# One piece or two for a pair's weighted sums, with the order of a whole kernel tuned anew

## The chip, the core and the metric

The kernel runs on one core of one Trainium2 chip. The metric is the device time of one execution in microseconds (us); lower is better. A core has TensorE (PE, matmuls; its weight loads are shown as PEld), VectorE (DVE), ScalarE (ACT), GpSimd (POOL) and SyncE (SP, which issues the DMAs here). TensorE writes its results to PSUM, eight banks of 512 fp32 columns on 128 partitions, from which ACT or DVE copies them out.

## The reference

Attention with a multiplicative decay comes first, over 8 batches and 8 heads, with 576 positions and 64 dimensions a head; then a gated layer over the 512 joined columns. All of it is fp32:

```python
scores = scale * np.matmul(q, k.transpose(0, 1, 3, 2))
decay = cum[:, :, :, None] - cum[:, :, None, :]        # cum: running sum of log f
scores = np.where(causal, -1000000000.0, scores + decay)
scores = scores - np.max(scores, axis=-1, keepdims=True)
attn = np.exp(scores)
attn = attn / (np.sum(attn, axis=-1, keepdims=True) + 1e-09)
x = attn @ v                                           # heads joined: (B, S, 512)
gate_pre = sum(conv_w[k] * x_shifted_by(4 - k) for k in range(5))
out = (1 / (1 + np.exp(-gate_pre)) * (x @ w_val)) @ w_out
```

The step of interest is `attn @ v`, the weighted sums of values.

## The kernel before

The 64 heads are taken as 32 pairs (two heads share the 128 partitions, 64 dimensions each); four pairs make a batch. For pair `i` five planning functions run in turn. `plan_t` transposes q and k on TensorE. `plan_s` multiplies them; for each block of rows VectorE adds the decay and finds the maximum (line 604), ScalarE takes the exponential with its row sum (line 608), and one of POOL, DVE or ACT divides by the sum (lines 380 and 382). Only blocks at or below the diagonal are computed. The first 512 rows go by four blocks of 128; the last 64 rows of both heads form one tile `Pl` of 576 columns, whose scores take two adjacent banks. `plan_pt` transposes the weights (lines 649, 667, 668), and copies them to the tiles `pt`. `plan_pv`, the changed function, multiplies the values `vt` with the transposed weights: head h goes to partitions 64h to 64h + 63, so each matmul uses half of the array's columns (128*64 in the trace). Its result x, 128 partitions by 576 positions, is copied to `x32` (class "X"), split in a rounded part `xh` and a rest `xl`, and used for the gate: for the first four pairs by matmuls with diagonal matrices ("CV"), then by five multiplications on VectorE ("conv", line 747). After four pairs `plan_moe` does the batch's sigmoid, the products with `w_val` (class "Mv", in three parts for precision), the product with the gate ("H", line 792), the products with `w_out` ("Mo") and the output copies and stores.

In `plan_pv` before, x is made in two parts, each with a bank of its own and a copy of its own. The first covers positions 0 to 383: 12 products of 128 columns over block rows 0 to 2. The second covers 384 to 575: eight products of 192 columns and two of 64. The profile counts two TensorE instructions for each of these fp32 products, hence 24 and 20. The first part needs the transposed weights named 1 and 2, the second those named 3, l and l4.

None of this is issued in the order in which it is written. Each piece of work is a node of a list (`Plan.add`) with its class, the engines that can do it and an assumed duration for each, its priority, and what it reads and writes. `Plan.order` (line 189) then plays the whole kernel through: again and again it picks the engine and node that can start first, taking from the nodes ready within a small slack (`SLACK`) the one with the lowest priority. The priority is the pair's number plus small steps (`prio`), plus an offset from the table `OFF` for the class and for one of six phases of the kernel (`phase`, line 92). `PEN` adds a penalty where a node could go to several engines; `STICK` favours TensorE work of the same array shape (`mode` 0 full array, 1 half of the rows, 3 half of the columns), and `SWITCH` is the assumed price of a change of shape. PSUM banks are given out here too: a node that first touches a bank waits in the plan until one is free, or two side by side where it asks for `width` 2 (`seize`, `room`), and a bank comes back 0.15 us after its last use. A node that takes a bank also waits for everything that later users of that bank wait for, unless it is marked loose (line 153). The result is one fixed sequence for each engine, kept on the chip; the actual waits there are those of each single instruction on its data and banks.

Of the kernel before, what the change touches and what calls it, by code (L numbers as in the profile page):

```python
# [15 lines left out]
P = 128  # L16
D = 64
S = 576
PAD = 64
W = PAD + S  # L20
NB = 4
# [16 lines left out]
SAME = {"PE": 0.0, "ACT": 0.06, "DVE": 0.1, "POOL": 0.1, "SP": 0.0, "DQ": 0.0}  # L38
SLACK = {"PE": 0.0, "ACT": 0.0, "DVE": 0.0, "POOL": 0.0, "SP": 0.1, "DQ": 0.2}
SWITCH = 0.105  # L40
STICK = 24.84
PORT = {"norm", "conv", "hh", "hl", "xl", "xh", "sel", "wv", "wo", "cw", "start", "st0", "cut0", "cuth", "cutl"}
TICK, BUSY = 10.24 / 3, 3150.0
OFF = {
# [13 lines left out]
    "norm": (-64.92, -34.44, -50.35, -154.2, -42.93, -56.64), "rec": (-34.14, 96.95, -10.49, -75.27, 12.83, -25.56),  # L58
    "red": (5.64, -89.32, -29.74, -47.57, -60.46, -12.2), "sel": (0.99, -66.53, -101.3, -61.6, -6.31, 30.49),
    "sig": (0.0, 0.0, 119.1, 276.6, 80.13, 83.28), "st0": (-101.2, 0.0, 0.0, 0.0, 0.0, 0.0),  # L60
    "start": (-51.51, 0.0, 0.0, 0.0, 0.0, 0.0), "tabD": (-58.73, 0.0, 0.0, 0.0, 0.0, 0.0),
# [4 lines left out]
}  # L66
PEN = {
# [5 lines left out]
    ("conv", "ACT"): (0.0, 0.0, 2.52, 7.5, 4.7, 2.58), ("conv", "DVE"): (0.0, 0.0, 0.38, 0.0, 0.0, 0.5),  # L73
    ("conv", "POOL"): (0.0, 0.0, 65.48, 22.89, 42.2, 42.68), ("cut0", "DVE"): (12.46, 0.0, 0.0, 0.0, 0.0, 0.0),
    ("diag", "DVE"): (0.33, 1.54, 0.91, 0.0, 0.0, 0.0), ("diag", "POOL"): (11.96, 28.56, 14.33, 0.0, 0.0, 0.0),
    ("hh", "ACT"): (0.0, 0.0, 0.06, 0.0, 0.0, 7.62), ("hh", "DVE"): (0.0, 0.0, 0.22, 12.6, 5.06, 1.54),
    ("hl", "DVE"): (0.0, 0.0, 9.17, 0.64, 3.65, 0.0), ("hl", "POOL"): (0.0, 0.0, 0.51, 0.54, 0.04, 22.01),
    ("load", "ACT"): (7.36, 0.0, 0.0, 0.0, 0.0, 0.0), ("load", "SP"): (0.03, 0.0, 0.0, 0.0, 0.0, 0.0),
    ("norm", "ACT"): (0.0, 0.04, 0.67, 0.05, 0.79, 15.64), ("norm", "DVE"): (0.77, 5.49, 22.53, 0.36, 6.39, 2.21),
    ("norm", "POOL"): (3.05, 17.25, 0.28, 44.42, 0.8, 0.08), ("sel", "DVE"): (29.3, 28.29, 53.65, 8.66, 76.26, 0.31),  # L80
    ("sel", "POOL"): (1.34, 0.0, 0.11, 0.0, 0.0, 9.64), ("start", "ACT"): (5.02, 0.0, 0.0, 0.0, 0.0, 0.0),
    ("start", "DVE"): (5.62, 0.0, 0.0, 0.0, 0.0, 0.0), ("start", "POOL"): (0.21, 0.0, 0.0, 0.0, 0.0, 0.0),
# [5 lines left out]
}  # L88
NONE = (0.0,) * 6

# [189 lines left out]
def tile_decay_attention_gated_mlp(  # L280
# [12 lines left out]
    B, H = q.shape[0], q.shape[1]  # L293
# [5 lines left out]
    T0 = KC - 1  # L299
# [14 lines left out]
    cw = const.tile([P, KC, G], F32, name="cw")  # L314
# [10 lines left out]
    pt = tiles(NH, [P, 1600], F32, "pt")  # L325
    vt = tiles(NQ, [P, NB + 1, 2, D], F32, "vt")
# [4 lines left out]
    xh = tiles(NX, [P, S], F32R, "xh")  # L331
    xl = tiles(NX, [P, S], F32R, "xl")
# [3 lines left out]
    hh = tiles(G, [P, W], F32R, "hh")  # L336
    hl = tiles(G, [P, W], F32R, "hl")
# [15 lines left out]
    new = plan.bank  # L353

    def bank(key):
        home = plan.home[key]
        return banks[:, 512 * home[0]:512 * (home[-1] + 1)]

    def mm(out, lhsT, rhs, start, stop):
        nc.tensor.matmul(out, lhsT=lhsT, rhs=rhs, start=start, stop=stop)  # L360
# [8 lines left out]
    dve, act, pool, pe = (one(e) for e in ("DVE", "ACT", "POOL", "PE"))  # L369

    def any_(cls, durs, prio, fn, reads=(), writes=(), **kw):
        return plan.add(cls, durs, prio, lambda e: fn(engine[e]), reads, writes, **kw)

    def copy(eng, out, in_):
        (eng.copy if eng is nc.scalar else eng.tensor_copy)(out=out, in_=in_)  # L375
# [13 lines left out]
    def ap(n):  # L389

        return {"ACT": n / 1200.0 + 0.05, "DVE": n / 960.0 + 0.075}
# [241 lines left out]
    def at(i, j):  # L633
        return 192 * j if i == 3 else (1152, 1280, 768)[i] + P * j
# [47 lines left out]
    def plan_pv(i):  # L682
        b, g = divmod(i, G)
        r = i % NQ
        ms = [(2 * i + h) % NH for h in range(2)]
        base = float(i) if i else -5.0
        xr = x32[r]
        vk = [("vt0", r), *(("vt", r, n) for n in range(3))]
        for half, (qa, qb) in enumerate(((0, 384), (384, 576))):
            key = new(("PV", i, half))  # L690
            p = base + 0.6 + 0.05 * half

            def go(key=key, half=half):
                t = bank(key)
                if half == 0:
                    for bq in range(3):
                        for j in range(bq + 1):
                            for h in range(2):
                                mm(t[D * h:D * h + D, P * bq:P * bq + P], vt[r][:, j, h], pt[ms[h]][:, at(bq, j):at(bq, j) + P], j == 0, j == bq)
                    return  # L700
                for j in range(NB):
                    for h in range(2):
                        mm(t[D * h:D * h + D, 0:192], vt[r][:, j, h], pt[ms[h]][:, 192 * j:192 * j + 192], j == 0, False)
                for h in range(2):
                    mm(t[D * h:D * h + D, P:192], vt[r][:, NB, h], pt[ms[h]][:, 1536:1600], False, True)
            names = ((1, 2), (3, "l", "l4"))[half]
            pe("PV", (1.36, 1.47)[half], p, go, [*vk, *(("pt", m, n) for m in ms for n in names), *(("pt0", m) for m in ms)], [key],
               cols=(6144, 7168)[half], mode=3)

            def ev(eng, key=key, qa=qa, qb=qb):  # L710
                copy(eng, xr[:, T0 + qa:T0 + qb], bank(key)[:, 0:qb - qa])
            any_("X", ap(qb - qa), p, ev, [key], [("x", r, half)])
        xv = xr[:, T0:]
        s = i % NX
        xk = [("x", r, 0), ("x", r, 1)]
        p = base + 0.8
# [224 lines left out]
```

## Time and profile before

| | us |
|---|---|
| median of three runs | 592.03 (588.51 to 593.89) |
| the profiled execution | 589.74 |
| its span, first to last instruction | 588.0 |
| TensorE busy | 566.3 |
| ScalarE busy | 460.9 |
| VectorE busy | 449.9 |
| GpSimd busy | 251.6 |

The profiled execution's time is 1.7 us more than its span. Busy time is the union of an engine's instructions; matmuls overlap one another, so a busy TensorE is not one at its peak. In a row of groups stand line, engine, operation, output and inputs, shape and count, then busy time, mean length in ns, idle time just before and what ended it. In rows of the timeline the first two numbers are start and length in us, `x44` counts merged instructions, and brackets hold the idle time before and its releaser. The granted clock of TensorE was 0.997 of full speed.

### The profile page before, as it was taken

The numbers are of one execution on the slowest core, as the hardware profiler recorded it, in microseconds if no ns is written. First come the engines' busy times: TensorE is split into PE (matmuls) and PEld (weight loads), VectorE is DVE, ScalarE is ACT, GpSimd is POOL, SyncE is SP. The second block draws the span as 40 slices with busy tenths as digits, with TensorE's granted clock in tenths as the row PEclk, the third lists the DMA queues.
The fourth block names the chain that finished last, engine by engine and source line by source line (L and its number), as shares of the span: only waits on it lengthen the run. The fifth ranks groups of instructions, "written<-read, shape, count | busy, mean of one in ns | idle before, by whom it ended". The sixth has DMA issues, their size and how long they took to land.

```text
span 588.0 us, 14152 instructions
## 1 busy us (share of the span) xinstructions
PE 566.3 (96%) x4773; PEld 493.8 (84%) x4773; DVE 449.9 (77%) x1200; ACT 460.9 (78%) x1252; POOL 251.6 (43%) x397
## 2 busy tenths in 40 slices
PE   6798989999999999999999999999999999999997
PEld 5576768888789988889888998989988998889995
DVE  5668969799987989779778888696767778775550
ACT  4979969999987698779898889987887786984201
POOL 5121257333322654553554654343664666371200
PEclk9999999999999999999999999999999999999999
DMA  5999787575754566385667666564666645210002
GB/s 136 258 223 262 167 232 220 155 180 158 232 134 137 147 186 192 116 236 145 174 160 194 173 178 178 166 179 124 171 200 171 169 131 163 81 47 19 37 37 89
DMA packets 136294, 93.44 MB, mean 159 GB/s; under 512 B 118474, under 2 KB 118494, under 8 KB 136222
## 3 DMA queue, kind: packets, MB, share of 16 engines
q1 hardware_dynamic: 136222, 92.54, 57.2%
q8 instruction: 38, 0.62, 0.5%
q14 instruction: 34, 0.28, 0.2%
HBM read 82.60 MB, written 9.91 MB: 157 GB/s over the span
## 4 chain that ended last, share of the span: by engine, by line
PE 70%; DVE 10%; ACT 7%; DMA 7%; issue 2%; SPq 2%; POOL 1%; DVEq 0%; POOLq 0%; ACTq 0%
PE banks L360 56%; PE banks L649 8%; DVE banks L604 4%; ACT P L608 3%; PE banks L530 3%; SPq L387 2%; DVE gate L747 2%; DMA vt<-in_v_dram 2%; PE banks L667 1%; DMA ot<-in_moe_w_out_dram 1%; ACT pt L375 1%; DMA dm<-decd 1%; DMA ot<-in_moe_w_val_dram 1%; DMA wu<-in_moe_w_val_dram 1%; DVE negm L604 1%
## 5 line engine op out<-in xcount | busy, mean ns | idle before, releaser
L608 ACT ACTIVATE P<-banks,negm 128x128 f32<-128x128 f32 (+3 forms) x256 | 132.9, 536 | 26.6 <-DVE negm L604 26.3
L604 DVE CUSTOM_DVE_ANT_0 banks<-banks,dm 128x128 f32<-128x128 f32 (+3 forms) x256 | 120.6, 515 | 30.3 <-PE banks L360 19.1
L375 ACT COPY pt<-banks 128x256 f32<-128x256 f32 (+2 forms) x320 | 115.9, 437 | 28.7 <-PE banks L649 24.2
L382 POOL TENSOR_SCALAR P<-P,rz 128x384 f32<-128x384 f32 (+3 forms) x134 | 79.7, 611 | 73.3 <-DVE rz L618 36.7
L360 PE MATMUL banks<-xh,wall 128*128 128x288 f32 x512 | 108.7, 299 | 1.5 <-ACT pt L375 1.4
L747 DVE SCALAR_TENSOR_TENSOR gate<-x,cw,gate 128x576 f32<-128x576 f32 x112 | 103.0, 920 | 1.8
L360 PE MATMUL banks<-pt,vt 128*64 128x128 f32 (+2 forms) x1408 | 97.0, 293 | 3.5 <-ACT pt L375 2.9
L360 PEld LDWEIGHTS banks<-pt,vt 128*64 128x64 f32 x1408 | 86.0, 138 | 15.6 <-ACT pt L375 4.3
L434 POOL TENSOR_SCALAR_AFFINE_SELECT dm<-dm 128x256 f32<-128x256 f32 x126 | 55.7, 467 | 96.6 <-DMA dm<-decd 90.2
L360 PE MATMUL banks<-wall,hh 128*128 128x512 f32 x288 | 93.0, 404 | 1.1 <-ACT P L608 0.9
L649 PE MATMUL banks<-ident,P 128*128 128x128 f32 x640 | 89.3, 277 | 4.0 <-ACT P L380 1.4
L360 PEld LDWEIGHTS banks<-xh,wall 128*128 128x128 f32 x512 | 83.5, 188 | 3.6 <-ACT pt L375 1.6
L649 PEld LDWEIGHTS banks<-ident,P 128*128 128x128 f32 x640 | 71.3, 140 | 12.2 <-ACT P L380 3.4
L360 PE MATMUL banks<-xl,wall 128*128 128x288 f32 x256 | 75.4, 295 | 0.0
L718 POOL TENSOR_TENSOR xl<-x,xh 128x576 fp32r<-128x576 f32 x32 | 50.6, 1583 | 48.9 <-ACT xh L375 48.9
L360 PEld LDWEIGHTS banks<-wall,hh 128*128 128x128 f32 x288 | 51.0, 188 | 11.7 <-ACT P L608 2.3
L360 PE MATMUL banks<-Xh 128*128 128x288 f32 (+4 forms) x280 | 58.4, 346 | 0.6 <-ACT P L608 0.5
L380 ACT ACTIVATE P<-P,rz 128x128 f32<-128x128 f32 (+3 forms) x114 | 58.2, 574 | 0.6 <-DVE rz L618 0.3
L360 PE MATMUL banks<-wall,hl 128*128 128x512 f32 x144 | 56.5, 392 | 0.0
L608 ACT ACTIVATION_READ_ACCUMULATOR P<-banks,negm 128x1 f32 x256 | 54.1, 211 | 0.0
L360 PE MATMUL banks<-Xh,Xl 128*128 128x288 f32 (+4 forms) x280 | 52.9, 314 | 0.0
L360 PE MATMUL banks<-Xl,Xh 128*128 128x288 f32 (+4 forms) x280 | 52.9, 313 | 0.0
(108 smaller groups left out, 933.3 us busy)
## 6 DMA issues: line engine op xcount, KB each, us to landing
dm<-decd SPq DMA_DIRECT2D x62, 640.0 KB, 5.9
out_dram<-ot SPq DMA_DIRECT2D x36, 256.0 KB, 2.3
dl<-decd SPq DMA_DIRECT2D x62, 144.0 KB, 3.7
qn<-in_q_dram SPq DMA_DIRECT2D x64, 128.0 KB, 2.8
kn<-in_k_dram SPq DMA_DIRECT2D x64, 128.0 KB, 6.3
vt<-in_v_dram SPq DMA_DIRECT2D x64, 128.0 KB, 3.1
zn<-in_q_dram SPq DMA_DIRECT2D x64, 16.0 KB, 3.1
zn<-in_k_dram SPq DMA_DIRECT2D x32, 32.0 KB, 2.8
```

The costliest lines, as they stand in the source:

```text
L360: nc.tensor.matmul(out, lhsT=lhsT, rhs=rhs, start=start, stop=stop)
L375: (eng.copy if eng is nc.scalar else eng.tensor_copy)(out=out, in_=in_)
L380: eng.activation(out=out, in_=in_, func=AF.Copy, scale=col)
L382: eng.tensor_scalar(out=out, in0=in_, scalar1=col, scalar2=0.0, op0=ALU.mult, op1=ALU.add)
L387: lambda e: (nc.sync if e == "SP" else nc.scalar).dma_start(out=out, in_=in_), reads, writes, **kw)
L434: nc.gpsimd.affine_select(out=t, in_=t, pattern=[[0, 2], [-1, P]], base=0, channel_multiplier=1, compare_op=ALU.is_ge, fill=-BIG)
L530: nc.tensor.transpose(out=bank(key)[:, n * P:(n + 1) * P], in_=src[:, n].rearrange("p h d -> p (h d)"), identity=ident)
L604: nc.vector.tensor_tensor_reduce(out=sl, in0=sl, in1=add[:, o:o + ext], op0=ALU.add, op1=ALU.min, scale=-0.125, scalar=3.0e38, accum_out=n ...
L608: nc.scalar.activation(out=dst[:, o:o + ext], in_=bank(key)[:, c0:c0 + ext], func=AF.Exp, bias=negm[r][:, col], scale=-1.0, accum_out=zs[r ...
L649: nc.tensor.transpose(out=bank(key)[:, c:c + P], in_=Pt[m][:, BOFF[b] + P * j:BOFF[b] + P * j + P], identity=ident)
L718: any_("xl", {"POOL": 1.4, "DVE": 0.67}, p, lambda eng: eng.tensor_tensor(out=xl[s], in0=xv, in1=xh[s][:, :].bitcast(F32), op=ALU.subtract ...
L747: eng.scalar_tensor_tensor(out=gt, in0=src, scalar=wt_, in1=gt, op0=ALU.mult, op1=ALU.add)
```

## The change

`plan_pv` makes one node of the two. It takes two adjacent banks and issues all products of the pair, the first part's and then the second's, to a view that starts at column 128 of the first bank: positions 0 to 383 fill that bank to its end, positions 384 to 575 the first 192 columns of the second. The node needs all transposed weights of the pair. One copy of 576 columns, for ACT or DVE, takes the place of the copies of 384 and 192. The assumed duration is 2.83 us, in place of 1.36 and 1.47. The numbers in `OFF`, `PEN` and `STICK`, which set the order, are replaced; a few rows of each table stand here, and the rest change in like manner. `PEN` gains entries such as ("CE", "ACT") and ("wo", "DVE") and loses ("conv", "DVE") and ("xh", "ACT").

```diff
-STICK = 24.84
+STICK = 23.54
...
-    "PT": (-42.2, 16.09, 19.11, 32.94, 6.68, 4.69), "PV": (-64.38, -24.3, 4.98, -25.87, -4.65, -72.64),
-    "S": (-48.98, -34.14, -48.85, -16.38, -24.39, -84.23), "SD": (146.1, 0.0, 0.0, 0.0, 0.0, 0.0),
-    "SX": (-75.7, -6.93, -12.7, 13.98, -13.66, 16.23), "T": (9.34, 83.08, -47.66, 3.31, -17.01, -77.97),
...
+    "PT": (-32.85, 31.08, 19.24, 34.11, -0.14, -0.33), "PV": (-75.34, -39.69, 2.88, -42.73, -13.14, -71.15),
+    "S": (-46.82, -37.29, -29.72, -8.51, -40.34, -65.96), "SD": (152.9, 0.0, 0.0, 0.0, 0.0, 0.0),
+    "SX": (-65.95, 2.57, 5.45, 27.72, -7.91, 13.86), "T": (-44.11, 47.99, -87.47, -36.81, -52.52, -90.14),
...
-        for half, (qa, qb) in enumerate(((0, 384), (384, 576))):
-            key = new(("PV", i, half))
-            p = base + 0.6 + 0.05 * half
-
-            def go(key=key, half=half):
-                t = bank(key)
-                if half == 0:
-                    for bq in range(3):
-                        for j in range(bq + 1):
-                            for h in range(2):
-                                mm(t[D * h:D * h + D, P * bq:P * bq + P], vt[r][:, j, h], pt[ms[h]][:, at(bq, j):at(bq, j) + P], j == 0, j == bq)
-                    return
-                for j in range(NB):
+        key = new(("PV", i), 2)
+
+        def go(key=key):
+            t = bank(key)[:, P:]
+            for bq in range(3):
+                for j in range(bq + 1):
                     for h in range(2):
-                        mm(t[D * h:D * h + D, 0:192], vt[r][:, j, h], pt[ms[h]][:, 192 * j:192 * j + 192], j == 0, False)
+                        mm(t[D * h:D * h + D, P * bq:P * bq + P], vt[r][:, j, h], pt[ms[h]][:, at(bq, j):at(bq, j) + P], j == 0, j == bq)
+            for j in range(NB):
                 for h in range(2):
-                    mm(t[D * h:D * h + D, P:192], vt[r][:, NB, h], pt[ms[h]][:, 1536:1600], False, True)
-            names = ((1, 2), (3, "l", "l4"))[half]
-            pe("PV", (1.36, 1.47)[half], p, go, [*vk, *(("pt", m, n) for m in ms for n in names), *(("pt0", m) for m in ms)], [key],
-               cols=(6144, 7168)[half], mode=3)
-
-            def ev(eng, key=key, qa=qa, qb=qb):
-                copy(eng, xr[:, T0 + qa:T0 + qb], bank(key)[:, 0:qb - qa])
-            any_("X", ap(qb - qa), p, ev, [key], [("x", r, half)])
+                    mm(t[D * h:D * h + D, 384:576], vt[r][:, j, h], pt[ms[h]][:, 192 * j:192 * j + 192], j == 0, False)
+            for h in range(2):
+                mm(t[D * h:D * h + D, 512:576], vt[r][:, NB, h], pt[ms[h]][:, 1536:1600], False, True)
+        pe("PV", 2.83, base + 0.65, go, [*vk, *(("pt", m, n) for m in ms for n in (1, 2, 3, "l", "l4")), *(("pt0", m) for m in ms)], [key],
+           cols=13312, mode=3)
+        any_("X", ap(S), base + 0.65, lambda eng, key=key: copy(eng, xr[:, T0:], bank(key)[:, P:P + S]), [key], [("x", r, 0), ("x", r, 1)])
```

More of the change, by code (lines that the diff above doesn't have):

```diff
@@ L44 @@
 OFF = {
[13 rows of a table removed]
[L58 to L61, printed above, removed]
[4 rows of a table removed]
[13 rows of a table added]
+    "norm": (-65.73, -57.4, -65.73, -164.1, -38.95, -65.45), "rec": (-58.37, 108.0, 10.25, -97.03, -2.44, -45.11),
@@ L66 @@
+    "red": (0.27, -73.65, -8.48, -64.28, -77.03, -3.12), "sel": (10.54, -34.61, -71.32, -48.15, 32.8, 54.18),
+    "sig": (0.0, 0.0, 98.36, 271.1, 101.0, 78.47), "st0": (-84.38, 0.0, 0.0, 0.0, 0.0, 0.0),
+    "start": (-69.3, 0.0, 0.0, 0.0, 0.0, 0.0), "tabD": (-41.76, 0.0, 0.0, 0.0, 0.0, 0.0),
[4 rows of a table added]
 }
 PEN = {
[5 rows of a table removed]
-    ("conv", "ACT"): (0.0, 0.0, 2.52, 7.5, 4.7, 2.58), ("conv", "DVE"): (0.0, 0.0, 0.38, 0.0, 0.0, 0.5),
-    ("conv", "POOL"): (0.0, 0.0, 65.48, 22.89, 42.2, 42.68), ("cut0", "DVE"): (12.46, 0.0, 0.0, 0.0, 0.0, 0.0),
@@ L75 @@
[L75 to L79, printed above, removed]
@@ L80 @@
-    ("norm", "POOL"): (3.05, 17.25, 0.28, 44.42, 0.8, 0.08), ("sel", "DVE"): (29.3, 28.29, 53.65, 8.66, 76.26, 0.31),
-    ("sel", "POOL"): (1.34, 0.0, 0.11, 0.0, 0.0, 9.64), ("start", "ACT"): (5.02, 0.0, 0.0, 0.0, 0.0, 0.0),
-    ("start", "DVE"): (5.62, 0.0, 0.0, 0.0, 0.0, 0.0), ("start", "POOL"): (0.21, 0.0, 0.0, 0.0, 0.0, 0.0),
[5 rows of a table removed]
[5 rows of a table added]
+    ("X", "DVE"): (2.13, 4.94, 35.86, 32.05, 0.71, 57.96), ("conv", "ACT"): (0.0, 0.0, 9.25, 9.3, 13.41, 4.22),
+    ("conv", "POOL"): (0.0, 0.0, 40.76, 4.31, 25.15, 41.53), ("cut0", "ACT"): (1.28, 0.0, 0.0, 0.0, 0.0, 0.0),
@@ new lines @@
+    ("cut0", "DVE"): (2.31, 0.0, 0.0, 0.0, 0.0, 0.0), ("diag", "DVE"): (0.92, 0.72, 0.04, 0.0, 0.0, 0.0),
+    ("diag", "POOL"): (16.29, 20.59, 11.74, 0.0, 0.0, 0.0), ("hh", "ACT"): (0.0, 0.0, 0.1, 0.14, 0.34, 0.75),
+    ("hh", "DVE"): (0.0, 0.0, 0.24, 8.42, 0.0, 0.0), ("hl", "DVE"): (0.0, 0.0, 8.88, 0.06, 5.67, 0.0),
+    ("hl", "POOL"): (0.0, 0.0, 0.31, 5.35, 0.65, 19.45), ("load", "ACT"): (4.84, 0.0, 0.0, 0.0, 0.0, 0.0),
+    ("norm", "ACT"): (0.0, 0.0, 0.83, 0.34, 1.19, 19.16), ("norm", "DVE"): (0.88, 7.08, 32.18, 0.41, 7.67, 8.27),
@@ L88 @@
+    ("norm", "POOL"): (6.91, 21.31, 0.17, 41.53, 0.77, 0.2), ("sel", "DVE"): (20.36, 31.89, 58.03, 8.15, 74.04, 11.84),
+    ("sel", "POOL"): (0.11, 0.9, 0.0, 0.01, 0.0, 0.0), ("start", "ACT"): (3.27, 0.0, 0.0, 0.0, 0.0, 0.0),
+    ("start", "DVE"): (5.56, 0.0, 0.0, 0.0, 0.0, 0.0), ("start", "POOL"): (1.17, 0.0, 0.0, 0.0, 0.0, 0.0),
[5 rows of a table added]
 }
```

48 rows, old and new, of tables (OFF, PEN) are left out of this document.

## The prediction

> **What bounds the kernel now.** I read the page first (busy shares and the chain), then the busy time by stage, then the groups that the change touches, then TensorE's own timeline around them, and last the waits and the tail.
>
> ```profile
> span 588.0 us, 14152 instructions
> PE 566.3 (96%) x4773; PEld 493.8 (84%) x4773; DVE 449.9 (77%) x1200; ACT 460.9 (78%) x1252; POOL 251.6 (43%) x397
> ...
> PE 70%; DVE 10%; ACT 7%; DMA 7%; issue 2%; SPq 2%; POOL 1%; DVEq 0%; POOLq 0%; ACTq 0%
> ```
>
> TensorE (PE) is the busiest engine and holds 70% of the chain that ended last. An average over stages can deceive, so the stages come next (columns: length, then busy time of each engine with its instruction count, then TensorE's granted clock, the DMA share, GB/s).
>
> ```profile
> 0.00:30.00 30.00, 21.50 (x148) 16.42 (x150) 18.75 (x52) 20.56 (x53) 9.36 (x31) 0.98 0.77 197
> 30.00:116.00 86.00, 80.58 (x624) 63.76 (x621) 68.08 (x206) 74.91 (x207) 34.31 (x59) 0.99 0.79 208
> 116.00:560.00 444.00, 439.95 (x3882) 392.78 (x3881) 355.49 (x923) 361.28 (x987) 207.95 (x307) 1.00 0.55 153
> 560.00:588.00 28.00, 24.27 (x127) 20.82 (x126) 7.59 (x21) 4.11 (x7) 0.00 (x0) 1.00 0.18 66
> ```
>
> There are two regimes. From 116 to 560 us TensorE is busy for 439.95 of 444.00 us at full clock, so 4.05 us of idle time is all that a better order could take from idling; ScalarE (ACT) and VectorE (DVE) are at 81% and 80% there and set nothing by their sums. Before 116 us TensorE idles 8.50 + 5.42 us, and ACT is busy for 74.91 of 86 us between 30 and 116. The last 28 us are matmuls of the output projection and the final copy and store.
>
> **The change part by part.** The work on the pair's weighted sums is in these groups (line 360 is the helper that issues all matmuls, line 375 the helper that copies; the last row is another copy by the same line, for its duration).
>
> ```profile
> L360 PE MATMUL banks<-pt,vt 128*64 128x128 f32 x768 | 49.1, 277 | 3.4 <-ACT pt L375 2.9 <-DVE gate L375 0.5
> L360 PE MATMUL banks<-pt,vt 128*64 128x192 f32 x512 | 48.7, 334 | 0.0
> L360 PE MATMUL banks<-pt,vt 128*64 128x64 f32 x128 | 9.3, 223 | 0.0
> L375 ACT COPY x<-banks 128x384 f32<-128x384 f32 x32 | 15.5, 483 | 7.3 <-PE banks L360 7.1
> L375 ACT COPY x<-banks 128x192 f32<-128x192 f32 x32 | 10.3, 323 | 10.7 <-PE banks L360 10.5
> L375 ACT COPY pt<-banks 128x512 f32<-128x512 f32 x128 | 74.4, 597 | 17.0 <-PE banks L649 16.3
> ```
>
> *Matmuls.* The diff issues the same products with the same operands and sizes: 24 + 20 instructions a pair (768/32, and (512 + 128)/32). The view starts at column 128 of the first bank, so the first 384 columns end exactly at the bank's end and the other 192 begin the second bank. No matmul is added or dropped; the term is 0. What can change is whether the two parts run back to back. TensorE's timeline (start, length, line, group, count) has both forms:
>
> ```profile
> 52.65 1.53 PE L360 MATMUL banks<-pt,vt 128*64 128x128 f32 x24 [0.53 <-DVE gate L375]
> 55.75 1.64 PE L360 MATMUL banks<-pt,vt 128*64 128x192 f32 x20
> ...
> 105.49 1.53 PE L360 MATMUL banks<-pt,vt 128*64 128x128 f32 x24
> 112.99 1.64 PE L360 MATMUL banks<-pt,vt 128*64 128x192 f32 x20
> ...
> 189.69 2.95 PE L360 MATMUL banks<-pt,vt 128*64 128x128 f32 x44
> ...
> 472.37 1.53 PE L360 MATMUL banks<-pt,vt 128*64 128x128 f32 x24
> 480.46 1.64 PE L360 MATMUL banks<-pt,vt 128*64 128x192 f32 x20
> ...
> 527.48 2.94 PE L360 MATMUL banks<-pt,vt 128*64 128x128 f32 x44
> ```
>
> Apart, the parts take 1.53 + 1.64 = 3.17 us, together 2.95: a split costs 0.22 us. But the order before already joins them in 27 of the 32 pairs. Only five are split: four between 52.65 and 112.99 us, and the one at 472.37. So "in one piece" is worth 1 x 0.22 us in the dense stage, and at most 4 x 0.22 = 0.88 us before 116 us.
>
> In those four early pairs the join can also cost. The first part now waits for what the second needs (the transposed weights 3, l and l4), so 1.5 us of work moves later, by up to 7.5 us (105.49 to 112.99), and leaves TensorE without that filler. If nothing else is ready it costs 4 x 1.53 = 6.1 us; if something is, nothing. TensorE idles in this stage anyway and other work is due in the same places, so the end near zero is nearer; I take the early splits at -0.4 us, with -0.9 and +6.1 as ends. In the dense stage 27 joins exist already, so the later start costs them nothing.
>
> *Copies.* Two copies a pair, 483 + 323 = 806 ns, become one of 576 columns. The two rows give (483 - 323)/192 = 0.83 ns a column, the 512-column copy takes 597, so 64 more make 650 ns. ACT loses 32 x 0.156 = 5.0 us of its 460.9 and 32 instructions. In the dense stage ACT is idle 19% of the time, so this hides under TensorE: 0. Before 116 us, where chains over ACT and VectorE do set the pace, it is worth at most 5 pairs x 0.16 = 0.8 us; I take -0.4.
>
> *x is complete later.* The first copy used to run under the second part's matmuls; now all of it follows the last matmul: 650 ns against 323, or 0.33 us later. What is queued behind is the cast to xh on ACT, the gate's first multiply on VectorE, xl on GpSimd. The place where that could reach the end is the last pair:
>
> ```profile
> 547.03 2.94 PE L360 MATMUL banks<-pt,vt 128*64 128x128 f32 x44
> 548.66 0.48 ACT L375 COPY x<-banks 128x384 f32<-128x384 f32 x1 [2.79 <-PE banks L360]
> 550.03 0.32 ACT L375 COPY x<-banks 128x192 f32<-128x192 f32 x1 [0.89 <-PE banks L360]
> 550.38 0.52 DVE L382 TENSOR_SCALAR gate<-x,cw 128x576 f32<-128x576 f32 x1 [1.90 <-ACT x L375]
> 551.13 1.92 POOL L718 TENSOR_TENSOR xl<-x,xh 128x576 fp32r<-128x576 f32 x1 [3.75 <-ACT xh L375]
> 555.40 0.69 ACT L763 ACTIVATE gate<-gate 128x576 f32<-128x576 f32 x1 [1.83 <-DVE gate L747]
> 555.63 0.29 PE L360 MATMUL banks<-xl,wall 128*128 128x288 f32 x1
> 556.49 0.46 DVE L792 TENSOR_TENSOR h<-banks,gate 128x288 f32<-128x288 f32 x1 [1.12 <-PE banks L360]
> ```
>
> xl ends at 553.05 and TensorE next takes an xl at 555.63: 2.6 us of cover. The gate is ready at 555.40 + 0.69 = 556.09 and its first user starts at 556.49, held by TensorE: 0.40 us of cover for 0.33. So 0; without that cover it is 0.33 us, once.
>
> *Banks.* A pair of banks must now be free side by side, from the first matmul to the end of the copy: about 2.95 + 0.7 = 3.65 us for two banks, 7.3 bank-us. Before, in the last pair, the first bank was held 547.03 to 549.14 (2.1 us), the second from about 548.5 to 550.35 (1.9 us): 4.0 bank-us. That is 3.3 bank-us more for each pair; between 189.69 and 527.48 us there are 22 pairs, one in 16.1 us, so of 8 banks x 16.1 = 129 bank-us it is 2.6%. Is TensorE short of banks now? Its waits from 116 to 560 us (total, times, longest) name copies only in crumbs, and they may be data as well as banks:
>
> ```profile
> PE banks L360 <- ACT P L608: 1.5, 6, 0.5
> ...
> PE banks L360 <- ACT pt L375: 0.2, 1, 0.2
> ```
>
> So banks cost nearly nothing before; a gain is excluded, since a longer hold frees no bank sooner, and the ends are 0 and one 597 ns copy awaited in every pair, 19 us. I take 0, being nearest to these rows. The Trainium skill, in "PSUM — Partial Sum Buffer", section "Summary: rules for kernel authors", says to evacuate promptly because the memory is tight. It speaks against holding two banks until both parts are done; by it the sum would move towards the third case below, while the waits above so far bear out little scarcity.
>
> *The new order.* Nearly every offset and penalty changes, most by a few units to a few tens. The trace of before can't show the new sequence. It can gain at most TensorE's idle time in the middle, 5.42 + 4.05 = 9.5 us, and some mode switches; it can lose as much if the list no longer fits the durations. I take 0.
>
> **Sum:** -0.2 (one split) -0.4 (early splits) -0.4 (early copies) + 0 = -1.0 us. On the profiled execution, 589.74 us with its 588.0 us span, that is 588.7. That execution is 2.3 us below the median of 592.03; the four times shown average 591.04. I forecast 591.04 - 1.0 = **590.0 us**.
>
> **The rivals.** What a measurement of this kernel can tell from no change is about 1%, 5.9 us.
>
> *A, no change that can be told (0.57).* As above; with the terms' smaller ends and the 588.51 to 593.89 us that the kernel before showed, 586 to 595.
>
> *B, faster by over 1% (0.27).* The new order takes most of the idle time: it must find 4.9 us beyond my 1.0. The 9.5 us of middle idling hold that, if over half of it goes. There is a second source:
>
> ```profile
> PEld banks L360 <- issue: 14.0, 68, 0.4
> ```
> ```profile
> 104.49 0.19 PEld L360 LDWEIGHTS banks<-Xh 64*128 64x128 f32 x2 [0.17 <-issue]
> ```
>
> These are gaps of 0.2 us (14.0/68) before weight loads, as the second row shows one where the array goes from full to half tiles. There are 68, of which the five splits can be only a few. Say 5 us of idling and 1 us of these: 590.0 - 6 = 584 us. For it: ACT has 5 us less to do in a stage where it is 87% busy (74.91 of 86). Against it: in the dense stage TensorE starts one matmul upon another and the change removes no matmul. The Trainium skill, in "Perfetto Trace Analysis", section "Identifying the Most-Contended Engine", holds matmul busy time a poor measure of headroom and wants the busy share of the weight loads, here 84% of the span and 88% (392.78 of 444.00) in the dense stage. By that, there would be 51 us to win in that stage. I don't raise B for it, since what fills those 51 us is matmuls that remain.
>
> *C, slower by over 1% (0.13).* Two adjacent banks come free late. One eviction of 597 ns then stands ahead of the pair's matmuls; in half of the pairs that is 16 x 0.6 = 9.6 us, 591.04 + 9.6 = 600.6 us. It decides from 5.9/32 = 0.18 us a pair. For it: 3.3 bank-us more a pair, and a part that before could begin with one bank free. Against it: another tile of the same width (the last 64 rows' scores) already gets its two banks, and TensorE's waits are small.
>
> *D, slower through the early join (0.03).* The 6.1 us of lost filler in full: 597 us.
>
> That the change does little of what it says is part of A: 27 of 32 pairs were in one piece.
>
> **How the numbers follow.** Faster is B, 0.27; same is A, 0.57; slower is C and D, 0.16. The likeliest case alone spans 586 to 595. The range for 8 in 10 goes down to 582, to leave out only B's far end (the whole 9.5 us and more), and up to 599, which holds D and the weaker half of C; about 0.08 lies beyond each side.
>
> **What would show it.** Right: 32 runs of 44 matmuls with 2.95 us each, 32 copies of 576 columns near 650 ns in place of 64, ACT's busy time near 456 us, TensorE's idle time between 116 and 560 us still 3 to 6 us. B would show as under 2 us of idling there or under 3 us between 30 and 116, with fewer of the 0.2 us gaps. C would show as TensorE waiting on a copy or an exponential just before the first of the 44, in ten or more pairs. The forecast is wrong if the middle idling moves by more than 5 us either way, or if the count of switches between array shapes changes by more than 30.

## The result and the profile after

The changed kernel takes 606.29 us (median; 606.09 to 607.57). Against the kernel before it is slower by a ratio of 1.0274, 95% interval 1.0233 to 1.0315, some 16 us. The forecast was 590.0 us in a range of 582 to 599: wrong, and outside the range.

First the page of the changed kernel: span, busy times and the shares of the chain that ended last.

```profile
span 605.9 us, 14110 instructions
PE 575.2 (95%) x4773; PEld 495.9 (82%) x4773; DVE 477.2 (79%) x1245; ACT 433.3 (72%) x1166; POOL 253.6 (42%) x406
PE 55%; DVE 23%; ACT 9%; DMA 6%; issue 5%; SPq 1%; POOL 0%; DVEq 0%; ACTq 0%
```

TensorE runs the same 4773 instructions, but its share of the chain has fallen from 70% to 55%, and VectorE's has risen from 10% to 23%. VectorE has 27.3 us more work than before (449.9), ScalarE 27.6 us less (460.9). VectorE is still idle for a fifth of the span.

The busy time by stage of the changed kernel, in the prediction's stages, then the stretch from 240 to 540 us alone (same columns as there):

```profile
0.00:30.00 30.00, 25.34 (x142) 18.32 (x144) 18.21 (x54) 20.70 (x56) 10.34 (x33) 0.94 0.78 205
30.00:116.00 86.00, 78.72 (x630) 62.50 (x627) 71.40 (x212) 72.82 (x198) 32.51 (x59) 1.00 0.82 220
116.00:560.00 444.00, 429.08 (x3743) 378.23 (x3743) 369.81 (x949) 326.62 (x892) 206.97 (x314) 1.00 0.54 149
...
240.00:540.00 300.00, 288.78 (x2527) 254.00 (x2526) 242.20 (x628) 215.64 (x585) 152.47 (x238) 0.99 0.55 155
```

The same stretch of the kernel before:

```profile
240.00:540.00 300.00, 298.01 (x2641) 266.31 (x2641) 236.42 (x627) 247.38 (x681) 153.23 (x229) 1.00 0.55 152
```

Up to 116 us TensorE has started 142 + 630 = 772 instructions, before 148 + 624 = 772: nothing is lost there. From 116 to 560 us it idles for 14.9 us where it idled for 4.05, and 11.2 us of that lie between 240 and 540 us, where before it was 2.0; it gets 114 instructions fewer done there. Beside the 10.9 us of idle time, its busy time over the whole span is 8.9 us longer for the same instructions. Several groups are a little longer (the weights' transposes 92.3 us for 89.3 before, the products with `xh` 110.5 for 108.7). That matmuls no longer start straight upon one another would do this, but no run shows it by itself.

The groups that the change touches, in the changed kernel:

```profile
L360 PE MATMUL banks<-pt,vt 128*64 128x128 f32 x768 | 49.0, 277 | 0.4 <-ACT Pl L608 0.4
L360 PE MATMUL banks<-pt,vt 128*64 128x192 f32 x512 | 47.0, 326 | 0.0
L375 ACT COPY x<-banks 128x576 f32<-128x576 f32 x14 | 8.9, 638 | 15.3 <-PE banks L360 14.0 <-POOL dm L434 1.1
L375 DVE COPY x<-banks 128x576 f32<-128x576 f32 x18 | 13.5, 748 | 25.2 <-PE banks L360 25.2
L739 DVE SCALAR_TENSOR_TENSOR gate<-x,cw,gate 128x576 f32<-128x576 f32 x112 | 109.9, 985 | 1.4
```

The weighted sums themselves wait for nothing: 0.4 us in 768 matmuls. On VectorE, where 18 of the 32 copies now run (pair 0 and pairs 11 to 27), the queue stands 25.2 us at the copies' waits for TensorE. One gate multiplication takes 985 ns on average, before 920.

About half of the 11.2 us between 240 and 540 us now lies ahead of the transposes of the weights. Its idle time ahead of tile P between 240 and 540 us by what ended it (us, times), first before, then after:

```profile
  ACT P L608: 0.3, 1
```
```profile
  ACT P L608: 5.0, 5
```

The exponential (line 608) ends these waits, and it waits in turn for VectorE's maximum. One place, on the timeline of the changed kernel (the row with `Xl,Xh` ends the score products of both heads for 512 columns):

```profile
503.40 2.94 PE L360 MATMUL banks<-pt,vt 128*64 128x128 f32 x44
506.46 0.76 DVE L375 COPY x<-banks 128x576 f32<-128x576 f32 x1 [2.99 <-PE banks L360]
506.84 0.40 PE L360 MATMUL banks<-Xl,Xh 64*128 64x512 f32 x2
507.25 0.52 DVE L382 TENSOR_SCALAR gate<-x,cw 128x576 f32<-128x576 f32 x1
507.69 0.69 DVE L604 CUSTOM_DVE_ANT_0 banks<-banks,dm 128x512 f32<-128x512 f32 x1
508.00 1.41 POOL L710 TENSOR_TENSOR xl<-x,xh 128x576 fp32r<-128x576 f32 x1 [1.29 <-ACT xh L375]
508.30 1.73 DVE L739 SCALAR_TENSOR_TENSOR gate<-x,cw,gate 128x576 f32<-128x576 f32 x1
509.95 0.69 DVE L604 CUSTOM_DVE_ANT_0 banks<-banks,dm 128x512 f32<-128x512 f32 x1
510.56 0.81 DVE L739 SCALAR_TENSOR_TENSOR gate<-x,cw,gate 128x576 f32<-128x576 f32 x1
510.73 0.69 ACT L608 ACTIVATE P<-banks,negm 128x512 f32<-128x512 f32 x1 [1.48 <-DVE negm L604]
511.56 1.53 PE L649 MATMUL banks<-ident,P 128*128 128x128 f32 x6 [1.60 <-ACT P L608]
```

VectorE stands 2.99 us at the copy of x, but that holds up little: the scores that the two maxima of 512 columns (line 604) read are done only by 507.24 us, and the copy ends at 507.22. What then stands ahead of the maxima is the gate: its first multiplication ahead of the one, a chained multiplication of 1.73 us between the two. ScalarE then waits 1.48 us for the second maximum, and TensorE 1.60 us for the exponential.

The starts and ends in the traces show the same for the whole stretch from 240 to 540 us. The score products of a pair come in two groups of blocks that these maxima read (512 and 256 columns, then 384 and 128). From the moment the first block of a group is done to its maximum, 19.3 us passed before, summed over 36 groups, and chained gate multiplications filled 6.1 of them. In the changed kernel 41.3 us pass in 34 groups: the gate multiplications fill 20.4, copies of x 0.6.

### The profile page after: what moved, and what is told of

It reads as the page before. It is cut to its first block, busy times and chain, and to the rows that moved or that the text cites. A ratio compares the mean times of both kernels' runs of the same rounds, so it can differ in the third digit from the quotient of the medians.

```text
span 605.9 us, 14110 instructions
## 1 busy us (share of the span) xinstructions
PE 575.2 (95%) x4773; PEld 495.9 (82%) x4773; DVE 477.2 (79%) x1245; ACT 433.3 (72%) x1166; POOL 253.6 (42%) x406
## 4 chain that ended last, share of the span: by engine, by line
PE 55%; DVE 23%; ACT 9%; DMA 6%; issue 5%; SPq 1%; POOL 0%; DVEq 0%; ACTq 0%
PE banks L360 44%; DVE banks L604 8%; PE banks L649 7%; DVE gate L739 5%; ACT P L608 4%; PE banks L530 2%; DMA kn<-in_k_dram 2%; DVE negm L604 2%; SPq L387 1%; PE banks L667 1%; DVE Xh L375 1%; ACT P L380 1%; DVE Xl L521 1%; DVE h L784 1%; DMA wu<-in_moe_w_val_dram 1%
## 5 line engine op out<-in xcount | busy, mean ns | idle before, releaser
L608 ACT ACTIVATE P<-banks,negm 128x512 f32<-128x512 f32 (+3 forms) x256 | 132.8, 532 | 39.9 <-DVE negm L604 39.6
L604 DVE CUSTOM_DVE_ANT_0 banks<-banks,dm 128x512 f32<-128x512 f32 (+3 forms) x256 | 120.4, 512 | 15.9 <-PE banks L360 5.3
L382 POOL TENSOR_SCALAR P<-P,rz 128x512 f32<-128x512 f32 (+3 forms) x148 | 87.6, 608 | 93.0 <-DVE rz L618 50.9
L360 PE MATMUL banks<-xh,wall 128*128 128x288 f32 x512 | 110.5, 301 | 2.2 <-ACT P L608 1.6
L739 DVE SCALAR_TENSOR_TENSOR gate<-x,cw,gate 128x576 f32<-128x576 f32 x112 | 109.9, 985 | 1.4
L649 PE MATMUL banks<-ident,P 128*128 128x128 f32 x640 | 92.3, 278 | 12.0 <-ACT P L608 7.1
L360 PE MATMUL banks<-pt,vt 128*64 128x128 f32 (+2 forms) x1408 | 94.2, 290 | 0.4 <-ACT Pl L608 0.4
L360 PE MATMUL banks<-Xh 128*128 128x288 f32 (+2 forms) x280 | 58.6, 347 | 2.7 <-ACT pt L375 1.1
L360 PE MATMUL banks<-Xh,Xl 128*128 128x288 f32 (+2 forms) x280 | 53.1, 314 | 0.0
L360 PE MATMUL banks<-Xl,Xh 128*128 128x288 f32 (+2 forms) x280 | 52.9, 313 | 0.0
L521 DVE TENSOR_TENSOR Xl<-banks,Xh 128x512 fp32r<-128x512 f32 (+1 forms) x84 | 47.9, 575 | 2.1
```

Source lines behind the costliest of these rows:

```text
L382: eng.tensor_scalar(out=out, in0=in_, scalar1=col, scalar2=0.0, op0=ALU.mult, op1=ALU.add)
L521: nc.vector.tensor_tensor(out=Xl[r][:, lo:lo + n], in0=bank(key)[:, 0:n], in1=Xh[r][:, lo:lo + n].bitcast(F32), op=ALU.subtract)
L604: nc.vector.tensor_tensor_reduce(out=sl, in0=sl, in1=add[:, o:o + ext], op0=ALU.add, op1=ALU.min, scale=-0.125, scalar=3.0e38, accum_out=n ...
L608: nc.scalar.activation(out=dst[:, o:o + ext], in_=bank(key)[:, c0:c0 + ext], func=AF.Exp, bias=negm[r][:, col], scale=-1.0, accum_out=zs[r ...
L649: nc.tensor.transpose(out=bank(key)[:, c:c + P], in_=Pt[m][:, BOFF[b] + P * j:BOFF[b] + P * j + P], identity=ident)
L739: eng.scalar_tensor_tensor(out=gt, in0=src, scalar=wt_, in1=gt, op0=ALU.mult, op1=ALU.add)
```

## The experiments

The change has two parts: the form (two banks, one run of matmuls, one copy) and the tables, which make another order. The theories differ in what they blame: the form in itself, the order in itself, or the two together, and within each a single wait or engine. To hold an order, some kernels carry the sequence of nodes, with engine and banks, written out as a list:

```diff
-    for fn, e in plan.order(BEGIN):
+    for fn, e in held(plan, HELD):
```

Where a form doesn't fit the list, 8 to 18 of its pieces are moved a few places; such a kernel is called a form in an order. Times are medians; the ratio is to the kernel before beside it (median 589.9 to 590.6 us).

### Form and order apart

The new `plan_pv` in the order of before:

> The order of before, written out and held on every engine, with the new form alone: one piece of 44 matmuls into two adjacent banks at the place of the second part, one copy of 576 columns at the place of the second copy; banks are given out anew. Theory 'the new order is at fault' (the form is harmless, as the prediction's sum had it): 589 to 594 us, no change. Theory 'two adjacent banks' (the form itself makes TensorE wait, the prediction's case C): 600 us or more, with TensorE idle 0.3 us or more ahead of many pairs' 44 matmuls.

The old `plan_pv`, two parts and two copies, in the new order:

> The order of the changed kernel, held on every engine, with the old form put back: two parts, a bank for each, two copies at the place of the one. Theory 'the new order is at fault': stays at 604 to 609 us. Theory 'two adjacent banks': falls to 590 to 596 us. If both have a share it lies between, near 600.

And each form with the other's tables, the order made anew from them (STICK, OFF and PEN alone exchanged):

> The old form with the new tables of offsets and penalties, list made anew. Theory 'the new order is at fault': about as slow as the changed kernel, 604 to 610 us. If the tables are good only for the form that they were tuned with, slower than both, 612 us or more. Theory 'two adjacent banks': near 592 us.

> The new form with the old tables, list made anew. If the form is harmless, 589 to 596 us. If the list reacts to any change of form and the tables fit one form only, far slower: 620 us or more, with the loss spread over stalls that have nothing to do with the weighted sums.

| | old order | new order |
|---|---|---|
| old form | 590.6 | 605.6, ratio 1.0254 (1.0201 to 1.0306) |
| new form | 601.6, ratio 1.0195 (1.0135 to 1.0255) | 606.3, ratio 1.0274 (1.0233 to 1.0315) |

The order alone costs nearly what both cost, the form alone some two thirds. In the old order the form costs 11 us; in the new order, undoing it wins 0.7. The new order costs the old form 15 us and the new form 5. So the two don't add, and each part is enough to lose most of the 16 us. The crossed tables give 625.2 (new tables, old form) and 646.2 us (old tables, new form), one execution each, at a granted clock of 0.983 and 0.959: both are slower than either kernel with its own tables, so neither set of tables serves the other form.

### What in the form costs, in the old order

One piece of the form at a time. The first part of the sums moved directly ahead of the second, banks and copies as before:

> The order of before held, old form with its two banks and two copies; only the first part of the weighted sums is moved, to stand directly ahead of the second part in every pair (27 pairs stood so already, and 12 pieces of other work move by a few places because their bank isn't free yet). It measures the late first part alone, the prediction's case D. If that is what cost 11 us with the new form in the old order: 598 to 604 us, with the loss before 116 us and near the 26th pair. If the two adjacent banks are: 590 to 593 us.

The copy of 384 moved directly ahead of the copy of 192, so that the first bank is held longer:

> The kernel before, order held, old form with single banks; only ScalarE's first copy (384 columns) is moved to stand directly ahead of the second. It measures a late x without any pair of banks. If the late copy costs: 594 to 598 us. If the pair of banks does: 589 to 592 us, as before.

Two adjacent banks, the two parts still separate in the order, with one copy:

```diff
-            key = new(("PV", i, half))
+        key = new(("PV", i), 2)
```

> The order of before held; both parts of the weighted sums stay at their own places, but write one pair of adjacent banks that must be free when the first begins, and one copy of 576 columns stands at the place of the second copy. It measures the banks and the late copy without the join. Theory 'two adjacent banks': 598 us or more, most of the 11 us, with TensorE idle ahead of the weighted sums. Theory 'late first part': 590 to 593 us.

The same banks with the two copies of before:

> As the run with the parts at their own places and one copy into a pair of adjacent banks, order of before held; but the two copies of 384 and 192 columns are back at their old places. The pair of banks is still taken together and given back together. If it is the pair of banks that costs the 6 us there (1.0101): 594 to 598 us again. If it is the one late copy: 590 to 592 us.

Two banks taken together by the first part and given back together by the second copy, but anywhere, not side by side:

```diff
+        both = [new(("PV", i, 0)), new(("PV", i, 1))]
-            key = new(("PV", i, half))
+            key = both[half]
```

> The order of before held, parts and copies at their old places and in old form, but a pair's two single banks are taken together when the first part begins and given back together after the second copy; they needn't lie side by side. Beside the run with two adjacent banks and two copies (595.3 us, 1.0111) it tells the side-by-side from the long hold. If lying side by side is what costs: 590 to 592 us. If taking two at once and holding them does: 594 to 597 us.

| in the old order | us | ratio, 95% |
|---|---|---|
| first part later | 593.05 | 1.0056 (1.0036 to 1.0076) |
| first copy later | 589.39 | 0.9991 (0.9967 to 1.0015) |
| adjacent banks, one copy | 595.37 | 1.0101 (1.0072 to 1.0131) |
| adjacent banks, two copies | 595.32 | 1.0111 (1.0058 to 1.0164) |
| two banks together, anywhere | 592.75 | 1.0055 (1.0023 to 1.0088) |

The later copy costs nothing, nor does it matter whether there is one copy or two. The later first part costs 3.3 us and the pair of adjacent banks 6.0 (its 595.37 us lie between the two times expected, as do the 592.75 of the two banks anywhere); their sum of 9.3 lies within the 8.0 to 15.1 us that the interval gives for the whole form. With the later first part TensorE has started 749 instructions by 116 us, before 772, so much of its price arises early. Where the banks' price arises shows in TensorE's idle time ahead of the products with `vt` from 116 us on (us, times, by what ended it); first adjacent banks with two copies, then the whole form, then two banks anywhere:

```profile
  ACT pt L375: 2.9, 5
  ACT Pl L608: 1.9, 2
```
```profile
  ACT pt L375: 3.2, 4
  ACT Pl L608: 2.0, 2
```
```profile
  ACT pt L375: 0.2, 1
```

With the banks side by side TensorE waits 4.8 to 5.2 us at the sums; without that condition it waits 0.2 us, as before, though two banks are held just as long. The lines name the copies and exponentials that ended the waits, which an instruction may need for its data or for a bank they held. The sums read nothing that an exponential writes, so those waits, 1.9 to 2.0 us, point to a bank. One pair on the timeline, before and with adjacent banks and two copies:

```profile
131.26 0.98 PE L360 MATMUL banks<-pt,vt 128*64 128x128 f32 x14 [0.17 <-ACT pt L375]
```
```profile
129.94 0.77 PE L360 MATMUL banks<-pt,vt 128*64 128x128 f32 x10 [1.35 <-ACT pt L375]
```

By the time alone the two cases aren't cleanly apart: their intervals overlap (1.0023 to 1.0088 and 1.0058 to 1.0164). By the medians, holding two banks together carries about half of the price, elsewhere than ahead of the sums; the intervals leave room for less, and for most of it. The traces can't settle the split either: the profiled execution took 597.48 us with two banks anywhere (median 592.75) and 592.81 us with adjacent ones (median 595.32).

### What in the new order costs

The new order gives VectorE 18 copies of x that ScalarE made before. In the new order with these copies back on ScalarE at the same places:

> The changed kernel with its order held; only the 18 copies of x that the new order gives to VectorE are made by ScalarE, at the same place in the program. VectorE loses about 13 us of work and the 25 us that it stood idle ahead of these copies. Theory 'the new order loads VectorE, and the exponentials wait behind it': 598 to 603 us in place of 606. Theory 'engine choice is harmless': 604 to 608 us.

The counterpart, the old order with 34 copies (pairs 11 to 27) moved to VectorE:

> The kernel before with its order held; only the 34 copies of x of pairs 11 to 27, where the new order gives them to VectorE, are made by VectorE, at the same place in the program. Theory 'the new order loads VectorE': 594 to 600 us. Theory 'engine choice is harmless': 589 to 593 us.

Then VectorE's own work cut, once in each order, by halving the width of four of the gate's five multiplications:

```diff
-                    eng.scalar_tensor_tensor(out=gt, in0=src, scalar=wt_, in1=gt, op0=ALU.mult, op1=ALU.add)
+                    eng.scalar_tensor_tensor(out=gt[:, 0:S // 2], in0=src[:, 0:S // 2], scalar=wt_, in1=gt[:, 0:S // 2], op0=ALU.mult, op1=ALU.add)
```

> The changed kernel, its order untouched; the gate's four chained multiplications on VectorE run over half of the columns only, so half of that part of the gate is left out. Every other instruction stands as it was. VectorE loses some 40 us of work, spread over pairs 4 to 31. Theory 'in the new order VectorE's queue stands ahead of the exponentials and so of TensorE': 606 falls to 598 us or less. Theory 'VectorE isn't what holds the new order; banks and TensorE's own sequence are': 603 us or more.

> The same cut in the kernel before, its order untouched: half of the columns of the gate's four chained multiplications are left out. TensorE is dense there, so under either theory it changes little: 586 to 590 us. What the new order gains beyond this is what VectorE costs in it.

And for contrast GpSimd's work cut, in the new order:

```diff
-                times(eng, sl, sl, rz[r][:, c:c + 1])
+                w = sl.shape[-1] // (2 if eng is nc.gpsimd else 1)
+                times(eng, sl[:, 0:w], sl[:, 0:w], rz[r][:, c:c + 1])
```

> The changed kernel, its order untouched; the divisions of weights by their row sums that GpSimd makes run over half of the columns, the other half stays undivided. GpSimd loses some 25 to 40 us of work. The new order gives GpSimd 14 more of these than the old one. Theory 'the weights come late from GpSimd, and TensorE waits with the transposes': 606 falls to 600 us or less. Otherwise 604 us or more.

| | us | ratio, 95% |
|---|---|---|
| new order, copies of x on ScalarE | 608.96 | 1.0323 (1.0294 to 1.0352) |
| old order, copies of x on VectorE | 591.81 | 1.0037 (1.0013 to 1.0060) |
| new order and form, half of the gate | 593.46 | 1.0056 (1.0035 to 1.0076) |
| old order and form, half of the gate | 587.56 | 0.9935 (0.9901 to 0.9968) |
| new order and form, half of GpSimd's divisions | 606.45 | 1.0272 (1.0239 to 1.0305) |

The same cut wins 12.8 us in the changed kernel and 2.6 us in the one before: about 10 of the 16 us lost pass through VectorE (9 by the ratios, with some 3 us either way by their intervals). The other 6 us are not explained by these runs. Halving the gate also took GpSimd's busy time from 253.6 to 242.3 us, but half of GpSimd's divisions, which took it to 227.0, win nothing. The gate itself might also come late for the product that reads it (h); the waits of TensorE that h ends are 1.2 us from 116 to 560 us in the changed kernel. Which engine copies x isn't it: moving the copies off VectorE wins nothing in the new order, where 608.96 us is longer than either theory gave, and moving them to VectorE costs 2 us in the old one. Nor is it the sum of VectorE's work. The stretch from 240 to 540 us in the old order with the copies on VectorE:

```profile
240.00:540.00 300.00, 297.72 (x2630) 264.73 (x2631) 246.37 (x657) 234.52 (x646) 157.10 (x233) 1.00 0.54 152
```

VectorE is busy for 246.37 us, more than the 242.20 of the changed kernel, and yet TensorE idles for 2.3 us, in the changed kernel for 11.2. The same stretch in the new order with the copies on ScalarE, then with half of the gate:

```profile
240.00:540.00 300.00, 289.94 (x2506) 254.36 (x2505) 231.58 (x618) 225.56 (x606) 149.93 (x236) 0.99 0.55 155
```
```profile
240.00:540.00 300.00, 295.80 (x2617) 263.51 (x2616) 231.57 (x658) 221.85 (x608) 148.85 (x245) 1.00 0.56 157
```

Both follow the new order, and VectorE is busy for 231.6 us in both, less than the 236.42 of the kernel before. Yet TensorE idles for 10.1 us in the one and 4.2 in the other, and gets 111 instructions fewer done in the one. VectorE's busy share thus goes with a stall or without one: what matters is which instructions stand ahead of the maximum of line 604 in its queue, and for how long. Counted as above, gate multiplications fill 21.5 us between a group's first block and its maximum with the copies on ScalarE, 7.7 with half of the gate, and 8.7 in the old order with the copies on VectorE. Halving the gate's instructions in that queue also takes 3 us off the waits ahead of the transposes; the idle time ahead of tile P from 240 to 540 us with half of the gate, and in the new order with the old form:

```profile
  ACT P L608: 2.0, 2
```
```profile
  ACT P L608: 4.6, 5
```

In the chain of the changed kernel with half of the gate VectorE is back at its old share, and TensorE too:

```profile
PE 71%; DVE 10%; ACT 9%; DMA 6%; issue 2%; POOL 1%; SPq 0%; DVEq 0%; POOLq 0%; ACTq 0%
```

In that kernel VectorE stood still longer at the copies of x than in the changed one (27.5 us for 25.2, in 11 waits each), so these waits alone don't make the loss.

### Whether a better order for the form is at hand

If the new order were only a poor one of many, other tables for the new form should do better. Tables found by small random steps from the new ones:

> The new form with other numbers in the tables of offsets and penalties, found by many small random steps from the changed kernel's own, each kept when the list came out shorter by its own assumed durations. The computation is the same. If the changed kernel's order is a poor one for its form, and not the form itself the cause: 596 to 602 us, clearly under 606, with less idling of TensorE ahead of the weights' transposes. If the form holds every order back: 604 us or more. Faster than the kernel before, 590, would need the form to cost nothing at all.

It takes 604.95 us, ratio 1.0263 (1.0221 to 1.0304). Its page, span and busy times:

```profile
span 602.0 us, 14145 instructions
PE 569.9 (95%) x4773; PEld 493.9 (82%) x4773; DVE 474.4 (79%) x1237; ACT 429.7 (71%) x1154; POOL 262.2 (44%) x426
```

It has the same tilt, 474.4 us on VectorE and 429.7 on ScalarE, and nearly the same loss. But these tables started from the new ones, so this is one more order of their kind, not a search of all. The best measured with the whole form stays 601.6 us, in the old order written out. No kernel here that computes the whole beats the one before: the later first copy, 589.39 us, can't be told from it.

## Why the prediction was wrong

**The step that failed is "The new order. ... I take 0".** Its own bounds said that it could gain at most 9.5 us and "can lose as much if the list no longer fits the durations"; only the gain was priced as a case (B). The new order alone cost 15 us, more than that bound. What the runs put in the place of that term is VectorE's queue: TensorE's idle time between 116 and 560 us went from 4.05 to 14.9 us, a rise beyond the 5 us that the prediction had set as its own refutation, about 10 us of the loss go when VectorE's gate work is halved, and the gate multiplications that stand between scores and their maxima grew from 6.1 to 20.4 us. The prediction had set VectorE aside with "81% and 80% there and set nothing by their sums". That was true of the sums, and beside the point: nothing in the sums says in which order a queue is worked off.

**"Banks ... I take 0" failed too, in the old order.** Two adjacent banks cost 6 us there, inside the stated ends of 0 and 19 us. Case C had the mechanism, priced at 9.6 us. But the evidence that it named, "TensorE waiting on a copy or an exponential just before the first of the 44, in ten or more pairs", is absent in the changed kernel, with 0.4 us in one wait: there the sums hardly wait, and the time goes elsewhere. So C came out on the right side and doesn't explain the changed kernel. That its 600.6 us lie near the 601.6 of the form in the old order is luck: the banks cost 6 us where C had 9.6, and the later first part added 3.3. Where C does show, it is in six or seven waits, not in half of the pairs.

**The early join, taken at -0.4 us with ends of -0.9 and +6.1, cost +3.3 us** (the later first part in the old order, for all five split pairs). Neither end held, 6.1 us "If nothing else is ready" or nothing "if something is": the join was covered in part. Case D's 6.1 us was the right mechanism at about twice its size. The prediction also passed over the fifth split: its first part moves from 472.37 us towards 480.46, in the dense stage, and with the later first part TensorE idles for 0.9 us from 460 to 500 us, where it idled for none.

**What held.** All 32 pairs run as 44 matmuls in 2.94 or 2.95 us; the group of 192 columns fell from 48.7 to 47.0 us. The copy of 576 columns takes 638 ns on ScalarE, predicted 650. The later copy is hidden, predicted 0, measured as a ratio of 0.9991. The count of switches between array shapes went from 228 to 222, within the 30 allowed. With the form in the old order ScalarE's busy time is 456.9 us, predicted 456. But the prediction left all copies on ScalarE: in the changed kernel 18 went to VectorE at 748 ns each, and ScalarE's busy time came to 433.3 us. The short gaps before the weight loads of line 360, which were to give case B 1 us, did go down:

```profile
PEld banks L360 <- issue: 11.6, 53, 0.5
```

Before, it was 14.0 us in 68. But such gaps before the loads of the transposes (line 649) rose from 1.3 to 3.1 us, so nothing was won.

**The share of weight loads.** The weight loads took 493.8 us of 588.0 before and 495.9 of 605.9 after: their share fell from 84 to 82% with the same 4773 loads while the kernel became slower. The Trainium skill, in "Perfetto Trace Analysis", section "Identifying the Most-Contended Engine", judges TensorE's headroom by that share. The prediction was right to expect no gain from that room; whether a better order could fill it, no run here shows.

**The chances.** Slower by over 1% had 0.16, all of it on the form. A case "the new order costs what its queues on ScalarE and VectorE now do to the transposes" was missing. The prediction saw the mechanism only before 116 us, where "chains over ACT and VectorE do set the pace", and nothing was lost there. An order that nobody has yet measured on the chip should have had a losing side at least as wide as its winning one.

**Left open.** Why the orders made for the new form both tilt work to VectorE and both end near 605 us; whether any order brings the form to 590 us; how the price of two banks splits between holding them together and having them side by side; and where some 6 of the 16 us go that stay when the gate is halved. For the rest, the halved gate and the traces point at the gate multiplications ahead of the maxima; a kernel that keeps the whole gate and only moves them behind the maxima was not run.

## What to carry to other kernels

Tables that steer an order belong to the form of the nodes with which they were made: here a change of form that adds no work cost two per cent in the old order, and the tables made anew for it did not win that back. So measure a new order before counting it as free. Judge an engine that works off a fixed queue by what stands ahead of the instructions that others wait for, not by its busy share: in 300 us, 242 us of work on VectorE went with 11.2 us of idle TensorE in one order, and 246 us with 2.3 us in another. Two banks side by side cost 6 us here, and TensorE waited for them; the same two banks anywhere cost 3 us, with intervals that overlap. Where the copy is hidden anyway, there is nothing to set against that price.

## What was not expected of the hardware

A gate multiplication on VectorE (line 739, 128x576) takes 0.8 us or up to 2.0. In the timeline above it takes 1.73 us beside GpSimd's `xl` of 508.00 to 509.41 us, and 0.81 us soon after. From 116 to 560 us in the changed kernel (minimum, median and maximum in ns):

```profile
L739 DVE SCALAR_TENSOR_TENSOR gate<-x,cw,gate x104: 779/817/2031, 115.9 to 545.6; 128x576 f32<-128x576 f32 x104
```

The median is near the 0.81 us. Of all 112, the 52 during which GpSimd does nothing take 0.78 to 0.82 us, the 20 that overlap most with an `xl` 1.36 us on average. The mean of 985 ns, 65 more than before, is 7 us more on VectorE over 112 instructions: an order also changes how long instructions take. The Trainium skill, in "GPSIMD Engine Reference", section "1. Specifications", says that GpSimd's interfaces to SBUF are shared with VectorE and contended by instructions with two SBUF inputs, as this one has. The trace agrees, with 1.73 us beside GpSimd's subtraction against the median of 0.82.
